# Moving a sum away from its products on VectorE, and holding back GpSimd's negations

## The chip, the cores and the metric

The kernel runs on one core of a Trainium2 chip. The metric is the device time of one execution in microseconds (us). Times are medians over several executions. A profile is one execution taken with the hardware profiler; its span is some 1.8 us shorter than the device time of the same execution.

Engines: PE is TensorE (matmuls), DVE is VectorE, ACT is ScalarE, POOL is GpSimd, SP issues DMAs.

## The reference, cut to what matters

```python
x = A_x                                              # 1 x 2048 x 576, bf16
# a 2-D Fourier filter of the normalised input, as a residual
X = rfft2(layernorm(x));  X = X * (w_r + 1j * w_i)   # 2048 x 289 complex weights
h = x + irfft2(X).astype(bf16)
# a gated feed-forward block of width 4608
h2 = h + (gelu(layernorm(h) @ w_gate) * (layernorm(h) @ w_up)) @ w_down
```

## The kernel before

The transforms are matmuls with tables. After a first stage (layer norm, table scaling, a transform along the 2048 axis) the data falls into 16 groups. In the loop over groups each group goes through five steps:

- D, on TensorE: the 576 axis, even and odd columns apart. ScalarE copies the even half out of PSUM.
- the butterfly, on VectorE: even + odd, then even - odd. Here called its sum part and its difference part.
- B, on TensorE: four-way combination of the two. ScalarE copies the result `YS` (real and imaginary plane) out of PSUM.
- the filter, on VectorE: two products of `YS` with planes of the weights `WS`, then their sum `ZS`. The first product needs a negated copy of the imaginary weights, plane 0 of `WS`. GpSimd makes these copies, one group at a time.
- V, on TensorE: the start of the inverse transform, from `ZS`. ScalarE copies the result out.

```python
def st_D(i):                      # group i: D, ScalarE's copy, then the butterfly
    ...                           # six matmuls into two banks, one ScalarE copy into ES
    P.op(DVE, ... CUS[:, s3, :, 0:HK] = e2 + o2 ...)             # L606
    P.op(DVE, ... CUS[:, s3, :, K2-1:HK-1:-1] = e2 - o2 ...)     # L607

def st_B(i):                      # group i: B, ScalarE's copy, then the filter
    ...                           # six matmuls, one ScalarE copy into YS
    for t_, w_ in enumerate((slice(1, None, -1), slice(2, 0, -1))):
        P.op(DVE, ... TP[:, sl, t_] = YS[:, sl] * WS[:, g, w_] ...)   # L629, two products
    P.op(DVE, ... ZS[:, z3] = TP[:, sl, :, 0] + TP[:, sl, :, 1] ...)  # L631, their sum

for i in range(NG):               # 16 negations on GpSimd, L665
    P.op(POOL, ... WS[:, g, 0, :] = WS[:, g, 2, :] * -1.0 ...,
         r=[imaginary weights of this half] + ["Wz"], w=[("Wn", i)])
for i in range(NG + 4):
    if i < NG:          st_D(i)
    if 2 <= i < NG + 2: st_B(i - 2)
    if i >= 4:          st_V(i - 4)
```

Each engine runs its own operations in program order. Between operations of one engine that depend on each other the program sets a semaphore wait; that holds for VectorE too. The imaginary weights arrive in two halves of eight groups, so the negations run in two blocks of eight. Right before the loop, VectorE scales the last four of sixteen table tiles (`ATS`, L472) and evicts the last results of the first stage (`U`, L505).

Of the kernel before, what the change touches and what calls it, by code (L numbers as in the profile page):

```python
# [7 lines left out]
ALU = mybir.AluOpType  # L8

S, D, K2 = 2048, 576, 289  # L10
KW = 290
# [3 lines left out]
NT = 16  # L15
NG = 16
# [279 lines left out]
def _build(nc, A_x, A_w_r, A_w_i, B_w_gate, B_w_up, B_w_down, out):  # L296
    P = Prog(nc)
    T = build_tables()
    dram = {n: nc.inline_tensor(_np_bf16(T[n]), name="c_" + n.lower()) for n in T}
    PE, DVE, ACT, SP, POOL = "pe", "dve", "act", "sp", "pool"  # L300
# [11 lines left out]
    WS = sb.alloc("WS", [128, NG, 3, KW], BF16)  # L312
# [34 lines left out]
    ATS = sb.alloc("ATS", [128, NT, 128], BF16)  # L347
# [7 lines left out]
    YS = sb.alloc("YS", [128, 2, 2, KW], BF16)  # L355
    t1_off = sb.off
    TP = sb.alloc("TP", [128, 2, 2, 2, KW], BF16)
    ZS = sb.alloc("ZS", [128, 3, 2, ZW], BF16)
# [11 lines left out]
    def bank(b, p0=0, p1=128, c0=0, c1=512):  # L370
        return PS[p0:p1, b * 512 + c0:b * 512 + c1]

    def banks(b, n, w):
        return PS[:, b * 512:(b + n) * 512].rearrange("p (a c) -> p a c", a=n)[:, :, 0:w]
# [41 lines left out]
    GORD = list(range(1, NG)) + [0]  # L416
    wkeys = [[("W", hf, pl, h) for pl in range(2) for h in range(8 + 2 * hf)] for hf in range(2)]
# [172 lines left out]
    def dbank(i):  # L590
        return 6 if i == 2 else 2 * ((i if i < 2 else i - 3) % 2)

    def st_D(i):
        g = GORD[i]
        sl, b0, s3 = i % 2, dbank(i), i % 3
        for o in range(2):
            b = b0 + o
            for dt in range(3):
                us = (2 * o + dt) if dt < 2 else 4
                P.op(PE, lambda t, b=b, o=o, dt=dt, us=us, g=g: t.matmul(bank(b, 0, 128, 0, 2 * HK), U[:, us, g, :, :], FT[:, o, dt, :],  # L600
                                                                        start=(dt == 0), stop=(dt == 2)),
                     r=uk[us] + ["FT"], w=[("PS", b)])
        P.op(ACT, lambda a, sl=sl, b0=b0: a.activation(ES[:, sl, :], bank(b0, 0, 128, 0, 2 * HK), ACTF.Copy), r=[("PS", b0)], w=[("E", sl)])
        e2 = ES[:, sl, :].rearrange("p (a b) -> p a b", a=2)
        o2 = bank(b0 + 1, 0, 128, 0, 2 * HK).rearrange("p (a b) -> p a b", a=2)
        P.op(DVE, lambda v, e2=e2, o2=o2, s3=s3: v.tensor_tensor(CUS[:, s3, :, 0:HK], e2, o2, op=ALU.add), r=[("E", sl), ("PS", b0 + 1)], w=[("CU", s3)])  # L606
        P.op(DVE, lambda v, e2=e2, o2=o2, s3=s3: v.tensor_tensor(CUS[:, s3, :, K2 - 1:HK - 1:-1], e2[:, :, 0:HK - 1], o2[:, :, 0:HK - 1], op=ALU.subtract),  # L607
             r=[("E", sl), ("PS", b0 + 1)], w=[("SU", s3)])

    LAST = NG - 1  # L610

    def st_B(i):
        g = GORD[i]
        sl = i % 2
        s3, sp_ = i % 3, 1 if g == 0 else 0
        b0 = {1: 6, LAST - 1: 2}.get(i, 4)

        for b, tabs in ((b0, (0, 1, 3)), (b0 + 1, (1, 2, 0))):
            for m, (tb, pl, q0, q1) in enumerate(((tabs[0], 0, 0, K2), (tabs[1], 1, 0, HK), (tabs[2], 1, HK, K2))):
                P.op(PE, lambda t, b=b, tb=tb, pl=pl, q0=q0, q1=q1, m=m, s3=s3, sp_=sp_: t.matmul(  # L620
                    bank(b, 0, 128, q0, q1), BT[:, sp_, tb, :], CUS[:, s3, pl, q0:q1], start=(m == 0), stop=(m == 2)),
                    r=[("CU", s3), ("SU", s3), "BT"], w=[("PS", b)])
        P.op(ACT, lambda a, sl=sl, b0=b0: a.activation(YS[:, sl, :, 0:K2], banks(b0, 2, K2), ACTF.Copy), r=[("PS", b0), ("PS", b0 + 1)], w=[("Y", sl)])  # L623
        wk = wkeys[0 if 1 <= g < 9 else 1] + [("Wn", i), "Yz", "Zz"]
        z3 = i % 3

        for q0, q1, hs in ((0, 128, (0,)), (128, KW, (1,))) if i == LAST else ((0, KW, (0, 1)),):
            for t_, w_ in enumerate((slice(1, None, -1), slice(2, 0, -1))):
                P.op(DVE, lambda v, sl=sl, g=g, q0=q0, q1=q1, t_=t_, w_=w_: v.tensor_tensor(TP[:, sl, t_, :, q0:q1], YS[:, sl, :, q0:q1], WS[:, g, w_, q0:q1], op=ALU.mult),  # L629
                     r=[("Y", sl)] + wk, w=[("T", sl, t_, h) for h in hs])  # L630
            P.op(DVE, lambda v, sl=sl, z3=z3, q0=q0, q1=q1: v.tensor_tensor(ZS[:, z3, :, q0:q1], TP[:, sl, :, 0, q0:q1], TP[:, sl, :, 1, q0:q1], op=ALU.add),  # L631
                 r=[("T", sl, t_, h) for t_ in range(2) for h in hs], w=[("Z", z3, h) for h in hs])


    VBANKS = {NG - 4: (0, 0, 1), NG - 2: (2, 2, 3), LAST: (0, 1, 4)}
# [1 line left out]
    def st_V(i):  # L637
        g = GORD[i]
        sl = i % 3
        sp_ = 1 if g == 0 else 0  # L640
        bs = VBANKS.get(i, (6, 6, 7))
        for c in range(3):
            b, o = bs[c], 256 if c == 1 and bs[0] == bs[1] else 0
            for zp in range(2):
                P.op(PE, lambda t, b=b, o=o, c=c, zp=zp, sl=sl, sp_=sp_: t.matmul(bank(b, 0, 128, o, o + 256), ZS[:, sl, zp, 128 * c:128 * c + 128],  # L645
                                                                                  VT[:, sp_, zp, :], start=(zp == 0), stop=(zp == 1)),
                     r=[("Z", sl, int(c > 0)), "Zz", "VT"], w=[("PS", b)])
            if i == LAST:
                src = bank(b, 0, 128, 0, 256).rearrange("p (k n e) -> p k n e", k=2, n=16)
                if c < 2:  # L650
                    P.op(DVE, lambda v, g=g, c=c, src=src: v.tensor_copy(V[:, 2 * c:2 * c + 2, :, g, :], src), r=[("PS", b), "Vfree"], w=[("V", g, c)])  # L651
                else:
                    P.op(ACT, lambda a, g=g, c=c, src=src: a.activation(V[:, 2 * c:2 * c + 2, :, g, :], src, ACTF.Copy), r=[("PS", b), "Vfree"], w=[("V", g, c)])
        if i < LAST:
            src = PS[:, bs[0] * 512:bs[0] * 512 + 768].rearrange("p (k n e) -> p k n e", k=6, n=16)
            P.op(ACT, lambda a, g=g, src=src: a.activation(V[:, :, :, g, :], src, ACTF.Copy), r=[("PS", bs[0]), ("PS", bs[2]), "Vfree"], w=[("V", g, c) for c in range(3)])  # L656

    def idle_ft(n, b):
        for _ in range(n):
            P.op(PE, lambda t, b=b: t.matmul(bank(b, 0, 128, 0, 2 * HK), FT[:, 0, 0, 0:128], FT[:, 0, 0, :], start=True, stop=True), r=["FT"], w=[("PS", b)])  # L660
# [2 lines left out]
    P.alias(["J0", "J1", "ZD"] + [(n_, c) for n_ in ("ATB", "ATS") for c in range(NT)], ["Vfree"])  # L663
    for i in range(NG):
        P.op(POOL, lambda v, g=GORD[i]: v.tensor_scalar(WS[:, g, 0, :], WS[:, g, 2, :], -1.0, None, op0=ALU.mult),  # L665
             r=[k for k in wkeys[0 if 1 <= GORD[i] < 9 else 1] if k[2] == 1] + ["Wz"], w=[("Wn", i)])
    for i in range(NG + 4):
        if i < NG:
            st_D(i)
        if 2 <= i < NG + 2:  # L670
            st_B(i - 2)
        if i == NG + 3:
            idle_ft(3, 5)
        if i >= 4:
            st_V(i - 4)
# [214 lines left out]
def bass_sequential_preLN__spectral_gfnet__geglu_ffn__prompt_kernel(  # L890
    nc, A_x, A_w_r, A_w_i, B_x, B_w_gate, B_w_up, B_w_down, out
):
    _build(nc, A_x, A_w_r, A_w_i, B_w_gate, B_w_up, B_w_down, out)
# [28 lines left out]
```

## Time and profile before

| | before |
|---|---|
| device time, first 3 runs | 504.44 us (504.13 to 504.98) |
| span of the profile | 502.9 us |
| first stage, ends with the first D matmul | 20.3 us |
| loop over groups | 20.3 to about 55 us |
| rest of the inverse transform | to about 77 us |
| gate, up and down matmuls | to the end |

The head of the page gives the busy time of each engine, its share of the span and its instructions; part 4 gives the chain of work that ended last, by engine.

```profile
span 502.9 us, 9972 instructions
PE 492.4 (98%) x4318; PEld 297.7 (59%) x4319; DVE 183.9 (37%) x391; ACT 158.7 (32%) x296; POOL 39.1 (8%) x49
...
PE 91%; DVE 6%; issue 1%; DMA 1%; ACT 1%; DVEq 0%
```

TensorE is busy nearly all the time, and the reader may stop there. But 6% of the chain, some 30 us, belongs to VectorE. Some 13 us of it lie in the first stage and some 17 us in the loop over groups. The next lines are VectorE's timeline of the kernel before, one group of the loop. The columns are start in us, length in us, engine, line, operation, output and inputs, shapes, count, and in brackets the idle time before it where there is any.

```profile
27.59 0.45 DVE L606 TENSOR_TENSOR CUS<-ES,PS 128x290 bf16<-128x290 f32 x1
27.96 0.45 DVE L607 TENSOR_TENSOR CUS<-ES,PS 128x288 bf16<-128x288 f32 x1
28.32 0.83 DVE L629 TENSOR_TENSOR TP<-YS,WS 128x580 bf16<-128x580 bf16 x2
29.18 0.47 DVE L631 TENSOR_TENSOR ZS<-TP 128x580 bf16<-128x580 bf16 x1
29.56 0.45 DVE L606 TENSOR_TENSOR CUS<-ES,PS 128x290 bf16<-128x290 f32 x1
```

Look at starts, not lengths. The butterfly's two parts start 0.37 us apart (27.59, 27.96), though each lasts 0.45 us: neighbours overlap. The two products end at 28.32 + 0.83 = 29.15 us, and the sum that reads them starts only then, at 29.18. A sum that could overlap would have started about 0.11 us earlier. This lost overlap, where an operation reads what the one right in front of it wrote, is called the drain below. One group takes 29.56 - 27.59 = 1.97 us, without a pause. This time from group to group is called the pitch.

TensorE needs 0.75 + 0.51 + 0.65 = 1.91 us for D, B and V of a group, read from starts where nothing holds it up. So in the middle of the loop VectorE is the tighter of the two by only 0.06 us. At the end of the loop, TensorE stands and waits for the sums (TensorE's timeline of the kernel before):

```profile
50.00 1.03 PE L645 MATMUL PS<-VT,ZS 128*128 128x256 bf16 x6 [0.64 <-DVE ZS L631]
50.87 0.67 PE L620 MATMUL PS<-CUS,BT 128*128 128x289 bf16 x6
51.97 0.82 PE L645 MATMUL PS<-VT,ZS 128*128 128x256 bf16 x6 [0.43 <-DVE ZS L631]
53.12 0.83 PE L645 MATMUL PS<-VT,ZS 128*128 128x256 bf16 x6 [0.33 <-DVE ZS L631]
```

The other place is the last table scaling before the loop. These lines are from VectorE's and GpSimd's timelines of the kernel before:

```profile
17.14 0.26 DVE L472 TENSOR_SCALAR ATS<-ATB,RS 128x128 bf16<-128x128 bf16 x1
17.60 0.79 DVE L472 TENSOR_SCALAR ATS<-ATB,RS 128x128 bf16<-128x128 bf16 x3 [0.21 <-issue]
17.75 0.97 POOL L665 TENSOR_SCALAR WS<-WS 128x290 bf16<-128x290 bf16 x1 [2.05 <-DMA WS<-in_A_w_i_dram]
```

The last three scalings take 0.79 us together, and there is a hole of 0.21 us before them. A negation on GpSimd starts at 17.75 us, when its weights land.

### The profile page before, as it was taken

What the parts mean: (1) busy time and instruction counts of PE and PEld (TensorE: products, weight loads), DVE (VectorE), ACT (ScalarE), POOL (GpSimd) and SP (SyncE); (2) the same over time, 40 slices, a digit from 0 to 9 for tenths busy, and PEclk for the clock granted to TensorE, in tenths of its full rate; (3) what the DMA queues carried; (4) which work ended last, traced back from release to release, by engine and by line L of the source; (5) the groups of instructions that cost most, each with busy time, mean ns of one, the idle gap of its engine ahead of it and who ended that gap; (6) DMA issues with size and microseconds to landing.
All of it is one profiled execution on the core that took longest, in us unless ns stands there. A gap on an engine that the chain in (4) does not pass through costs nothing.

```text
span 502.9 us, 9972 instructions
## 1 busy us (share of the span) xinstructions
PE 492.4 (98%) x4318; PEld 297.7 (59%) x4319; DVE 183.9 (37%) x391; ACT 158.7 (32%) x296; POOL 39.1 (8%) x49
## 2 busy tenths in 40 slices
PE   6899999999999999999999999999999999999998
PEld 2687674444458764444477744444577644444775
DVE  5899673344431114343310134333201233333111
ACT  7888776653220003333200023323100133323000
POOL 3644281000000000000000000000000000000000
PEclk9999999999999999999999999999999999999999
DMA  8779789001100000100000001100000000000000
GB/s 284 165 224 334 235 292 353 6 4 25 25 5 13 18 19 17 22 17 1 2 7 18 19 15 23 22 4 1 1 18 19 13 1 1 1 2 2 12 19 19
DMA packets 25948, 28.64 MB, mean 57 GB/s; under 512 B 11568, under 2 KB 19888, under 8 KB 25776
## 3 DMA queue, kind: packets, MB, share of 16 engines
q1 hardware_dynamic: 23328, 17.39, 12.1%
q0 software_dynamic: 2576, 10.62, 6.3%
q8 instruction: 34, 0.56, 0.5%
q14 instruction: 10, 0.08, 0.1%
HBM read 23.66 MB, written 2.36 MB: 52 GB/s over the span
## 4 chain that ended last, share of the span: by engine, by line
PE 91%; DVE 6%; issue 1%; DMA 1%; ACT 1%; DVEq 0%
PE PS L838 56%; PE PS L861 28%; PE PS L700 3%; DVE TP L629 2%; PE PS L739 2%; PE PS L600 1%; DVE ST L440 1%; DVE CUS L606 1%; PE PS L645 1%; DVE CUS L607 1%; DMA XO<-in_A_x_dram 1%; PE PS L620 1%; DVE U L505 0%; DVE ATS L472 0%; ACT JNK L431 0%
## 5 line engine op out<-in xcount | busy, mean ns | idle before, releaser
L838 PE MATMUL PS<-HT,WGU 64*128 64x512 bf16 x2592 | 281.9, 376 | 0.0
L838 PEld LDWEIGHTS PS<-HT,WGU 64*128 64x128 bf16 x2592 | 137.3, 94 | 143.4 <-issue 1.2
L850 ACT ACTIVATE GL<-PS 128x512 bf16<-128x512 f32 x144 | 85.9, 597 | 289.3 <-PE PS L838 289.3
L851 DVE TENSOR_TENSOR AT<-GL,PS 128x512 bf16<-128x512 bf16 x144 | 99.0, 688 | 174.1 <-PE PS L838 172.5
L861 PE MATMUL PS<-WD,AT 128*128 128x288 bf16 (+2 forms) x1152 | 141.8, 286 | 0.0
L861 PEld LDWEIGHTS PS<-WD,AT 128*128 128x128 bf16 x1152 | 111.0, 98 | 31.5 <-issue 1.7
L864 DVE TENSOR_TENSOR OS<-PS,XO 128x288 bf16<-128x288 f32 (+2 forms) x32 | 14.7, 458 | 125.8 <-PE PS L861 125.8
L665 POOL TENSOR_SCALAR WS<-WS 128x290 bf16<-128x290 bf16 x16 | 15.2, 949 | 9.3 <-DMA WS<-in_A_w_i_dram 8.2
L742 DVE SCALAR_TENSOR_TENSOR XO<-PS,XO 128x576 bf16<-128x576 f32 x16 | 12.1, 756 | 8.4 <-PE PS L739 8.4
L645 PE MATMUL PS<-VT,ZS 128*128 128x256 bf16 x96 | 13.4, 272 | 1.7 <-DVE ZS L631 1.4
L600 PE MATMUL PS<-FT,U 128*128 128x290 bf16 x96 | 14.4, 287 | 0.5 <-DVE U L505 0.5
L700 PE MATMUL PS<-DT,V 128*128 128x289 bf16 x96 | 14.6, 287 | 0.2 <-DVE V L651 0.2
L629 DVE TENSOR_TENSOR TP<-YS,WS 128x580 bf16<-128x580 bf16 (+2 forms) x34 | 13.5, 438 | 0.3 <-issue 0.3
L656 ACT ACTIVATE V<-PS 128x768 bf16<-128x768 f32 x15 | 12.2, 811 | 2.1 <-PE PS L645 1.8
L623 ACT ACTIVATE YS<-PS 128x578 bf16<-128x578 f32 x16 | 10.5, 655 | 3.3 <-PE PS L620 3.3
L494 PE MATMUL PS<-ATS,XO 128*128 128x128 bf16 (+1 forms) x80 | 7.1, 223 | 4.4 <-POOL ATS L467 2.7
L709 ACT ACTIVATE GS<-PS 128x578 bf16<-128x578 f32 x15 | 9.8, 655 | 4.2 <-PE PS L700 4.1
L645 PEld LDWEIGHTS PS<-VT,ZS 128*128 128x128 bf16 x96 | 8.1, 97 | 4.8 <-DVE ZS L631 1.0
L600 PEld LDWEIGHTS PS<-FT,U 128*128 128x128 bf16 x96 | 9.2, 98 | 3.0 <-issue 0.7
L700 PEld LDWEIGHTS PS<-DT,V 128*128 128x128 bf16 x96 | 8.9, 97 | 3.4 <-DVE V L651 0.4
L730 ACT ACTIVATE OS<-XO 128x576 bf16<-128x576 bf16 x16 | 10.8, 675 | 0.0
L620 PE MATMUL PS<-CUS,BT 128*128 128x289 bf16 (+2 forms) x96 | 10.7, 247 | 0.0
(58 smaller groups left out, 158.6 us busy)
## 6 DMA issues: line engine op xcount, KB each, us to landing
WD<-in_B_w_down_dram POOLq DMA_DIRECT2D x9, 576.0 KB, 8.3
WGU<-in_B_w_up_dram SPq DMA_DIRECT2D x4, 1152.0 KB, 9.6
WGU<-in_B_w_gate_dram POOLq DMA_DIRECT2D x4, 1152.0 KB, 10.4
out_dram<-OS SPq DMA_DIRECT2D x30, 72.0 KB, 1.6
XO<-in_A_x_dram SPq DMA_DIRECT2D x3, 576.0 KB, 6.9
IT<-c_itab SPq DMA_DIRECT2D x1, 1024.0 KB, 7.0
HT<-HN SPq DMA_TRANSPOSE x60, 2.4
XO<-in_A_x_dram SPq DMA_DIRECT2D x2, 288.0 KB, 3.2
```

The lines of the kernel that those rows point to most:

```text
L600: P.op(PE, lambda t, b=b, o=o, dt=dt, us=us, g=g: t.matmul(bank(b, 0, 128, 0, 2 * HK), U[:, us, g, :, :], FT[:, o, dt, :], start=(dt == 0) ...
L620: P.op(PE, lambda t, b=b, tb=tb, pl=pl, q0=q0, q1=q1, m=m, s3=s3, sp_=sp_: t.matmul(bank(b, 0, 128, q0, q1), BT[:, sp_, tb, :], CUS[:, s3, ...
L629: P.op(DVE, lambda v, sl=sl, g=g, q0=q0, q1=q1, t_=t_, w_=w_: v.tensor_tensor(TP[:, sl, t_, :, q0:q1], YS[:, sl, :, q0:q1], WS[:, g, w_, q ...
L645: P.op(PE, lambda t, b=b, o=o, c=c, zp=zp, sl=sl, sp_=sp_: t.matmul(bank(b, 0, 128, o, o + 256), ZS[:, sl, zp, 128 * c:128 * c + 128], VT[ ...
L656: P.op(ACT, lambda a, g=g, src=src: a.activation(V[:, :, :, g, :], src, ACTF.Copy), r=[("PS", bs[0]), ("PS", bs[2]), "Vfree"], w=[("V", g, ...
L665: P.op(POOL, lambda v, g=GORD[i]: v.tensor_scalar(WS[:, g, 0, :], WS[:, g, 2, :], -1.0, None, op0=ALU.mult), r=[k for k in wkeys[0 if 1 <= ...
L700: P.op(PE, lambda t, b=b, h=h, i=i, kt=kt, c=c: t.matmul(bank(b, 0, 128, 0, K2), V[:, kt, c, :, :], DT[:, 3 * h + i, 0:K2], start=(i == 0) ...
L838: op = P.op(PE, lambda t, h0=h0, kt=kt, wt=wt, f=f, b=b, HT=HT, s=(half == 0 and j in (0, 5)), e=(half == 1 and j in (3, 8)): t.matmul(ban ...
L850: P.op(ACT, lambda a, s2=s2, b0=b0: a.activation(GL[:, s2, :], bank(b0), ACTF.Gelu_apprx_tanh), r=[("PS", b0)], w=[("GL", s2)])
L851: P.op(DVE, lambda v, s2=s2, b0=b0, f=f: v.tensor_tensor(AT[:, f, :], GL[:, s2, :], bank(b0 + 1), op=ALU.mult), r=[("GL", s2), ("PS", b0 + ...
L861: P.op(PE, lambda t, b=b, d0=d0, d1=d1, f=f, p=p: t.matmul(bank(b, 0, 128, 0, d1 - d0), AT[:, f, 128 * p:128 * p + 128], WD[:, f, d0:d1], ...
L864: P.op(DVE, lambda v, b=b, d0=d0, d1=d1, p=p, c=c: v.tensor_tensor(OS[:, p % 2, d0:d1], bank(b, 0, 128, 0, d1 - d0), XO[:, c, d0:d1], op=A ...
```

## The change

It has two parts. First, the sum of group i-3 goes between the butterfly's two parts of group i, so that it no longer follows the product it reads. The end of the loop is reordered in the same spirit. Second, GpSimd's negations must wait until the last table tile is scaled.

```diff
-        (butterfly at the end of st_D)
+    def st_U(i):
         P.op(DVE, ... CUS[:, s3, :, 0:HK] = e2 + o2 ...)
+        if i >= 3:
+            st_Z(i - 3)
         P.op(DVE, ... CUS[:, s3, :, K2-1:HK-1:-1] = e2 - o2 ...)
-        (products and sum at the end of st_B)
+    def st_T(i, t_, ...):   # one product
+    def st_Z(i, ...):       # the sum
...
     for i in range(NG):
         P.op(POOL, ... WS[:, g, 0, :] = -WS[:, g, 2, :] ...,
-             r=[...] + ["Wz"], w=[("Wn", i)])
+             r=[...] + ["Wz", ("ATS", NT - 1)], w=[("Wn", i)])
     for i in range(NG + 4):
         if i < NG:
             st_D(i)
+            st_U(i)
+        if i == NG:
+            st_Z(NG - 3)
         if 2 <= i < NG + 2:
             st_B(i - 2)
+        if 2 <= i <= NG:
+            st_T(i - 2, 0)
+            st_T(i - 2, 1)
+        if i == NG + 1:
+            (products of the last group by halves, between them the last two groups' sums)
         ...
```

No operation is added or removed.

More of the change, by code (lines that the diff above doesn't have):

```diff
@@ L603, in st_D @@
         P.op(ACT, lambda a, sl=sl, b0=b0: a.activation(ES[:, sl, :], bank(b0, 0, 128, 0, 2 * HK), ACTF.Copy), r=[("PS", b0)], w=[("E", sl)])
+    def st_U(i):
+        sl, b0, s3 = i % 2, dbank(i), i % 3
         e2 = ES[:, sl, :].rearrange("p (a b) -> p a b", a=2)
@@ L623, in st_B, with st_T, st_Z @@
         P.op(ACT, lambda a, sl=sl, b0=b0: a.activation(YS[:, sl, :, 0:K2], banks(b0, 2, K2), ACTF.Copy), r=[("PS", b0), ("PS", b0 + 1)], w=[("Y", sl)])
-        wk = wkeys[0 if 1 <= g < 9 else 1] + [("Wn", i), "Yz", "Zz"]
-        z3 = i % 3
-        for q0, q1, hs in ((0, 128, (0,)), (128, KW, (1,))) if i == LAST else ((0, KW, (0, 1)),):
-            for t_, w_ in enumerate((slice(1, None, -1), slice(2, 0, -1))):
-                P.op(DVE, lambda v, sl=sl, g=g, q0=q0, q1=q1, t_=t_, w_=w_: v.tensor_tensor(TP[:, sl, t_, :, q0:q1], YS[:, sl, :, q0:q1], WS[:, g, w_, q0:q1], op=ALU.mult),
-                     r=[("Y", sl)] + wk, w=[("T", sl, t_, h) for h in hs])
-            P.op(DVE, lambda v, sl=sl, z3=z3, q0=q0, q1=q1: v.tensor_tensor(ZS[:, z3, :, q0:q1], TP[:, sl, :, 0, q0:q1], TP[:, sl, :, 1, q0:q1], op=ALU.add),
-                 r=[("T", sl, t_, h) for t_ in range(2) for h in hs], w=[("Z", z3, h) for h in hs])
+    def st_T(i, t_, q0=0, q1=KW, hs=(0, 1)):
+        g, sl = GORD[i], i % 2
+        w_ = (slice(1, None, -1), slice(2, 0, -1))[t_]
+        P.op(DVE, lambda v: v.tensor_tensor(TP[:, sl, t_, :, q0:q1], YS[:, sl, :, q0:q1], WS[:, g, w_, q0:q1], op=ALU.mult),
+             r=[("Y", sl), ("Wn", i), "Yz", "Zz"] + wkeys[0 if 1 <= g < 9 else 1], w=[("T", sl, t_, h) for h in hs])
+    def st_Z(i, q0=0, q1=KW, hs=(0, 1)):
+        sl, z3 = i % 2, i % 3
+        P.op(DVE, lambda v: v.tensor_tensor(ZS[:, z3, :, q0:q1], TP[:, sl, :, 0, q0:q1], TP[:, sl, :, 1, q0:q1], op=ALU.add),
+             r=[("T", sl, t_, h) for t_ in range(2) for h in hs], w=[("Z", z3, h) for h in hs])
     VBANKS = {NG - 4: (0, 0, 1), NG - 2: (2, 2, 3), LAST: (0, 1, 4)}
@@ L665, in _build @@
         P.op(POOL, lambda v, g=GORD[i]: v.tensor_scalar(WS[:, g, 0, :], WS[:, g, 2, :], -1.0, None, op0=ALU.mult),
-             r=[k for k in wkeys[0 if 1 <= GORD[i] < 9 else 1] if k[2] == 1] + ["Wz"], w=[("Wn", i)])
+             r=[k for k in wkeys[0 if 1 <= GORD[i] < 9 else 1] if k[2] == 1] + ["Wz", ("ATS", NT - 1)], w=[("Wn", i)])
     for i in range(NG + 4):
@@ L669, in _build @@
             st_D(i)
+            st_U(i)
+        if i == NG:
+            st_Z(NG - 3)
         if 2 <= i < NG + 2:
             st_B(i - 2)
+        if 2 <= i <= NG:
+            st_T(i - 2, 0)
+            st_T(i - 2, 1)
+        if i == NG + 1:
+            st_T(LAST, 0, 0, 128, (0,))
+            st_Z(LAST - 1)
+            st_T(LAST, 1, 0, 128, (0,))
+            st_T(LAST, 0, 128, KW, (1,))
+            st_Z(LAST, 0, 128, (0,))
+            st_T(LAST, 1, 128, KW, (1,))
+            st_Z(LAST, 128, KW, (1,))
         if i == NG + 3:
```

## The prediction

> **What bounds the kernel now.** The page gives TensorE 98% of a 502.9 us span; its chain is 91% TensorE, 56% and 28% of it the gate/up and down matmuls, which the change does not touch. Only the spectral filter, about 20.3 to 55.6 us, can gain. There the chain of waits runs on VectorE from 33.7 to 54.6 us. In the timeline one group takes VectorE five operations: butterfly sum, butterfly difference, two filter products, their sum. Independent neighbours start 0.37 us apart though each lasts 0.45 us: they overlap by 0.08 us. The sum, which waits for the second product, starts only 0.03 us after that one's end. So a group takes 1.97 us (27.59, 29.56, 31.53 us) and VectorE has no idle time. TensorE needs, undisturbed, 0.75 + 0.51 + 0.65 = 1.91 us per group, ScalarE less.
>
> The Trainium skill, "VectorE: DVE Perf Modes", section "The DRAIN you can't avoid", says that the next operation waits for the pipe to empty and that a semaphore costs nothing. This trace differs: 0.37 us between independent starts, 0.48 us where the next reads the result.
>
> **What the change does.** It removes no work. It puts the sum of group i-3 between two operations that do not depend on it, so the drain of about 0.11 us goes, once per group: VectorE 1.97 -> 1.86 us. Then TensorE is the limit, 1.91 us, so in the steady state 0.06 us per group is won on TensorE's side, while VectorE catches up. The second inverse-stage operand comes one group later, about 0.15 us once at the start; later there is slack. In the tail (48.7 to 55.2 us), where TensorE waits 0.64 + 0.43 + 0.33 us for the sums, VectorE's lead counts in full: 16 drains x 0.11 = 1.8 us. Sum for the loop: about 1.8 us.
>
> Second part: GpSimd's negations start at 17.75 us, beside the last four table scalings on VectorE. These take 17.14 to 18.39 us with a hole of 0.21 us, one of them 0.456 us; the first ones took 0.25 us at a pitch of 0.17. Undisturbed: 0.76 instead of 1.25 us. The chain runs through them (scalings, evictions, first filter matmul at 20.33 us), so about 0.4 us. The negations then start near 18 us; their first user is at 24 us, so they are not late. The Trainium skill, "SBUF — State Buffer", section "SBUF: two separate sides", describes an exclusive lock between GpSimd and VectorE operations with two SBUF inputs or in a two-port mode. The trace agrees in direction, not in a full block: the sum takes 0.56 to 0.62 us beside the second block of negations (32.0 to 40.2 us), 0.46 us without, and groups take 2.07 us there. That block waits for a DMA, so it stays; I expect still some 2.0 us per group there.
>
> **On the critical path:** both parts, fully; from 55 us on the matmul stages are bound by TensorE and should only shift. 1.8 + 0.4 = 2.2 us, less a little for new hitches: 2.1 us, 504.44 -> 502.3 us. Range 501.5 to 503.7. Faster by over 2% would need 10 us: chance 0.005; within 2%: 0.99; slower: 0.005.
>
> **What would show it.** Sums no longer 0.48 us after the second product; groups at 1.91 us on TensorE from 26 to 32 and 41 to 47 us, VectorE with small gaps; first filter matmul near 19.9 us; last sum ends near 52.2 instead of 54.6 us; first gate/up matmul near 74.6 instead of 76.8 us; everything after unchanged in length.
>
> **What would make it wrong.** Negations blocking the sums or products longer at their new place; the scaling's hole having another cause; TensorE now waiting for the later sum in every group; ScalarE's queue delaying the tail; weight loads arriving too late for the earlier start.

## More of the kernel before

One run of the kernel before, of 574.59 us, was slow and is left out everywhere.

## The result, and the profile after

| | before | after |
|---|---|---|
| device time, 4 runs each | 504.71 us (504.13 to 505.09) | 502.91 us (502.74 to 503.11) |
| first D matmul | 20.33 us | 20.17 us |
| first V matmul | 25.85 us | 25.73 us |
| V of the twelfth group | 48.04 us | 47.11 us |
| last filter sum ends | 54.63 us | 52.82 us |
| first gate/up matmul | 76.72 us | 75.03 us |
| span of the profile | 502.9 us | 501.2 us |

The ratio is 0.9965, with a 95% interval of 0.9948 to 0.9983. A ratio here is the mean time of one kernel's runs over that of the other's runs of the same rounds, so it is not quite the ratio of the medians quoted. Executions over 1.5% slower than the fastest of the same kernel are left out of the means. The interval excludes 1: 1.8 us are gained.

The table shows where, for these two profiles. 0.16 us come before the loop, of which 0.04 are lost again up to the first V. These 0.16 us need not be the change's: in the profile of order_only below, which has no new wait, the first D began at 20.11 us, and in that of wait_only at 19.98 us. Between the first V and the twelfth 0.81 us are gained, from there to the last sum another 0.88 us. After the loop everything moves along: the first gate/up matmul is 1.69 us earlier and the span 1.7 us shorter.

The page's head after:

```profile
span 501.2 us, 9972 instructions
PE 492.9 (98%) x4319; PEld 299.5 (60%) x4319; DVE 182.5 (36%) x391; ACT 158.4 (32%) x296; POOL 39.8 (8%) x49
...
PE 90%; DVE 7%; issue 1%; DMA 1%; SPq 0%; ACT 0%; DVEq 0%
```

It tells next to nothing: a gain of 0.35% does not show in shares. VectorE's timeline of the kernel after, one group, does:

```profile
28.60 0.44 DVE L610 TENSOR_TENSOR CUS<-ES,PS 128x290 bf16<-128x290 f32 x1
28.97 0.45 DVE L640 TENSOR_TENSOR ZS<-TP 128x580 bf16<-128x580 bf16 x1
29.34 0.44 DVE L613 TENSOR_TENSOR CUS<-ES,PS 128x288 bf16<-128x288 f32 x1
29.71 0.81 DVE L635 TENSOR_TENSOR TP<-YS,WS 128x580 bf16<-128x580 bf16 x2
30.45 0.44 DVE L610 TENSOR_TENSOR CUS<-ES,PS 128x290 bf16<-128x290 f32 x1
```

All five operations now start 0.37 us after the one before. A group takes 30.45 - 28.60 = 1.85 us, 0.12 us less. TensorE waits less at the end of the loop, 0.22 + 0.35 + 0.47 us where it waited 0.64 + 0.43 + 0.33 us:

```profile
48.66 0.83 PE L654 MATMUL PS<-VT,ZS 128*128 128x256 bf16 x6 [0.22 <-DVE ZS L640]
49.32 0.67 PE L626 MATMUL PS<-CUS,BT 128*128 128x289 bf16 x6
50.35 0.82 PE L654 MATMUL PS<-VT,ZS 128*128 128x256 bf16 x6 [0.35 <-DVE ZS L640]
51.63 0.83 PE L654 MATMUL PS<-VT,ZS 128*128 128x256 bf16 x6 [0.47 <-DVE ZS L640]
```

Before the loop, the three scalings are back at 0.58 us and the negation starts after them. The hole of 0.2 us is still there, with nothing running on GpSimd:

```profile
17.20 0.25 DVE L472 TENSOR_SCALAR ATS<-ATB,RS 128x128 bf16<-128x128 bf16 x1
17.65 0.58 DVE L472 TENSOR_SCALAR ATS<-ATB,RS 128x128 bf16<-128x128 bf16 x3 [0.19 <-issue]
...
18.39 0.97 POOL L674 TENSOR_SCALAR WS<-WS 128x290 bf16<-128x290 bf16 x1 [2.63 <-DVE ATS L472]
```

### The profile page after: what moved, and what is told of

Same layout as the page of the kernel before. It is cut to its first block, busy times and chain, and to the rows that moved or that the text cites. A ratio compares the mean times of both kernels' runs of the same rounds, so it can differ in the third digit from the quotient of the medians.

```text
span 501.2 us, 9972 instructions
## 1 busy us (share of the span) xinstructions
PE 492.9 (98%) x4319; PEld 299.5 (60%) x4319; DVE 182.5 (36%) x391; ACT 158.4 (32%) x296; POOL 39.8 (8%) x49
## 4 chain that ended last, share of the span: by engine, by line
PE 90%; DVE 7%; issue 1%; DMA 1%; SPq 0%; ACT 0%; DVEq 0%
PE PS L861 56%; PE PS L884 28%; PE PS L723 3%; DVE TP L635 2%; PE PS L762 2%; DVE ST L440 1%; DMA XO<-in_A_x_dram 1%; DVE ZS L640 1%; DVE CUS L613 1%; PE PS L600 1%; DVE U L505 0%; SPq L206 0%; PE PS L807 0%; PE PS L654 0%; DVE CUS L610 0%
## 5 line engine op out<-in xcount | busy, mean ns | idle before, releaser
L762 PE MATMUL PS<-GS,IT 128*128 128x288 bf16 x64 | 10.5, 285 | 0.0
L483 PE MATMUL PS<-ZD 128*128 128x512 bf16 x24 | 9.1, 537 | 1.3 <-POOL ZD L377 1.3
```

Of the source, the lines that this page charges most:

```text
L762: P.op(PE, lambda t, b=b, h=h, i=i, c=c, rhs=rhs: t.matmul(bank(b, 0, 128, 0, 288), IT[:, h * i, c, :], rhs, start=(i == 0), stop=(i == 1) ...
```

## The experiments

Twelve kernels ran, in three sets; each set shares its runs of the kernel before (medians of the fast ones 504.60, 504.57 and 504.81 us). All gave the right result but one.

| kernel | device time, median | ratio to before, 95% interval |
|---|---|---|
| order_only | 502.95 us | 0.9967 (0.9955 to 0.998) |
| wait_only | 504.62 us | 0.9997 (0.9984 to 1.001) |
| drain_back | 504.15 us | 0.999 (0.9978 to 1.0003) |
| sum_after_difference | 502.99 us | 0.9968 (0.9954 to 0.9981) |
| no_negation (wrong result) | 502.19 us | 0.9953 (0.994 to 0.9965) |
| batched_negation | 507.16 us | 1.0051 (1.0037 to 1.0065) |
| vector_negation | 502.85 us | 0.9967 (0.9954 to 0.9979) |
| four_extra_ops | 502.93 us | 0.9968 (0.9954 to 0.9981) |
| late_sum_from_8 | 503.29 us | 0.9966 (0.9953 to 0.9979) |
| late_sum_and_half_on_vector | 502.39 us | 0.9956 (0.9942 to 0.997) |
| vector_negation_fewer | 502.79 us | 0.9963 (0.995 to 0.9976) |
| early_plane (one run) | 503.18 us | not timed |

### Each part alone: order_only and wait_only

order_only is the kernel after without the new wait:

```diff
-             r=[...] + ["Wz", ("ATS", NT - 1)], w=[("Wn", i)])
+             r=[...] + ["Wz"], w=[("Wn", i)])
```

> The new order of VectorE's operations alone, the negations free to start as before. Theory D (the sum no longer waits for the drain of the product right before it): nearly all of the gain is here, about 1.5 of 1.8 us, so about 503.1 us against 504.7; the group's pitch on VectorE where GpSimd is idle is 1.84 us instead of 1.97. Rival P (the gain comes from GpSimd's negations starting later, so that they no longer disturb VectorE): no more than 0.3 us here, about 504.4 us.

wait_only is the kernel before with that wait:

```diff
-             r=[...] + ["Wz"], w=[("Wn", i)])
+             r=[...] + ["Wz", ("ATS", NT - 1)], w=[("Wn", i)])
```

> The old order with the negations made to wait for the last table scaling. Theory D: about 0.2 us, as the chain from the first scaling of the last group (17.20 us) to the first filter matmul (20.17 us) took 2.97 us after the change and 3.19 before; total about 504.5 us, pitch of a group 1.97 us where GpSimd is idle. Rival P: most of the 1.8 us, about 503.1 us. The forecast of 0.4 us for this part fails if the hole of 0.2 us between the first two of these scalings is still there.

The order alone gives 502.95 us, the whole gain as far as these runs can tell. The wait alone gives 504.62 us, nothing that these runs can see; the interval would hide some 0.2 us. Rival P falls. In the profile of order_only the weights landed a little later than in that of before, at 18.14 us, as the last scaling ended (18.17 us). So there was nothing for the wait to prevent. The pitch of a group where GpSimd is idle was 1.84 us in order_only and 1.97 us in wait_only, as expected. In wait_only the hole was there too, and its first negation started later, at 18.21 us. VectorE's and GpSimd's timelines of order_only:

```profile
17.59 0.58 DVE L472 TENSOR_SCALAR ATS<-ATB,RS 128x128 bf16<-128x128 bf16 x3 [0.21 <-issue]
18.14 8.47 POOL L674 TENSOR_SCALAR WS<-WS 128x290 bf16<-128x290 bf16 x8 [2.45 <-DMA WS<-in_A_w_i_dram]
```

VectorE's timeline of wait_only:

```profile
17.46 0.58 DVE L472 TENSOR_SCALAR ATS<-ATB,RS 128x128 bf16<-128x128 bf16 x3 [0.19 <-issue]
```

### The drain put back: drain_back

The second product of group i-3 is moved right in front of its sum. The sum keeps its new place in the loop.

```diff
         if i >= 3:
+            st_T(i - 3, 1)
             st_Z(i - 3)
...
         if i == NG:
+            st_T(NG - 3, 1)
             st_Z(NG - 3)
...
             st_T(i - 2, 0)
-            st_T(i - 2, 1)
+            if i == NG:
+                st_T(i - 2, 1)
```

> The kernel after the change, with the second product of group i-3 moved to stand right in front of its sum, between the butterfly's two parts. The sum keeps its new place and its lateness, but again reads what the operation right before it wrote. Theory D: the drain is back, the pitch is 1.95 to 1.97 us where GpSimd is idle, and the time about 504.4 us, like wait_only. Rival O (the place of the sum matters: later for TensorE, between two operations that read PSUM): the pitch stays 1.84 us and the time 502.9 us.

VectorE's timeline of drain_back, one group (L636 is a product, L641 the sum, L610 and L614 the butterfly):

```profile
28.23 0.46 DVE L610 TENSOR_TENSOR CUS<-ES,PS 128x290 bf16<-128x290 f32 x1
28.60 0.46 DVE L636 TENSOR_TENSOR TP<-YS,WS 128x580 bf16<-128x580 bf16 x1
29.09 0.46 DVE L641 TENSOR_TENSOR ZS<-TP 128x580 bf16<-128x580 bf16 x1
29.47 0.45 DVE L614 TENSOR_TENSOR CUS<-ES,PS 128x288 bf16<-128x288 f32 x1
29.83 0.46 DVE L636 TENSOR_TENSOR TP<-YS,WS 128x580 bf16<-128x580 bf16 x1
30.20 0.45 DVE L610 TENSOR_TENSOR CUS<-ES,PS 128x290 bf16<-128x290 f32 x1
```

Here product and sum stand apart and can be read singly. Every start is 0.36 to 0.38 us after the one before, but the sum starts 29.09 - 28.60 = 0.49 us after its product, at the product's end. The group is back at 1.97 us and the time at 504.15 us. From the first D to the last sum the loop took 53.95 - 19.95 = 34.00 us, as in wait_only (34.07 us), against 32.46 us in order_only. Rival O, that the place of the sum matters, falls. The 0.45 us by which the time is under before lie within the interval of the timing, so nothing is read from them.

The semaphore wait as such is not what costs. In the trace of the kernel after, the sum still carries a wait for VectorE's own semaphore, but for a product that ended earlier, and it starts 0.37 us after its neighbour. What costs 0.11 us is to wait for the operation right in front.

### Another independent neighbour: sum_after_difference

```diff
         P.op(DVE, ... even + odd ...)
-        if i >= 3:
-            st_Z(i - 3)
         P.op(DVE, ... even - odd ...)
+        if i >= 3:
+            st_Z(i - 3)
```

> The kernel after the change, with the sum of group i-3 behind the butterfly's difference instead of in front of it. It depends on neither. Theory D: any independent neighbour will do, the pitch stays 1.84 us and the time is within 0.3 us of 502.9. Rival O: the place between the two parts matters, so the gain shrinks by half or more, 503.8 us or over. Beside the negations the three operations with two SBUF inputs now stand in a row; if the lost time is per first one of such a row, the group beside the second block of negations gets no slower than 1.98 us.

502.99 us: another independent neighbour does as well. The pitch is 1.84 us. The profile showed something else, though. While the second block of negations ran, VectorE kept this pitch from 32.1 to 39.5 us, as if GpSimd were not there, and the eight negations took 11.36 us where they take 8.81 us in the kernel after. Here the time was lost on GpSimd's side. That led to the third set. What was won there was lost elsewhere in the same profile: the first V started at 25.84 us, 5.93 us after the first D; in the kernel after it was 25.73 - 20.17 = 5.56 us.

### What the negations still cost: no_negation

The negations are left out, and the first product reads a plane of right shape and wrong sign. The relative error was 0.042.

```diff
-    for i in range(NG):
-        P.op(POOL, ... negation ...)
...
-        w_ = (slice(1, None, -1), slice(2, 0, -1))[t_]
+        w_ = (slice(1, 3), slice(2, 0, -1))[t_]
...   (GpSimd's weight loads: r=list(wkeys[1]) added)
```

> Wrong result on purpose: the kernel after the change with GpSimd's 16 negations left out (the first product reads a plane of right shape and wrong sign; GpSimd's weight loads are tied to the second half of the filter's imaginary plane, so that they start near 32 us). It sizes what the negations still cost after the change. Theory C (they still hold up VectorE, 0.88 us in all beside five groups in the profile after, 0.73 of it in the second block): the pitch is 1.84 us until TensorE bounds it at 1.91, and the time falls by 0.5 to 0.8 us to about 502.2. Rival T (TensorE at 1.91 us per group bounds the stage already, so VectorE's lost time is slack): within 0.2 us of 502.9.

502.19 us, and all five runs lie within 0.06 us. So the negations cost the changed kernel 502.91 - 502.19, about 0.7 us (medians of two sets). In the profiles 0.61 us of it lie in the loop: from the first D to the last sum it took 32.04 us, against 32.65 us. Theory C holds. In this profile TensorE runs at 1.91 us per group through the whole loop, and after the first groups VectorE waits for ScalarE's copy only once, near 50 us.

### One long negation: batched_negation

```diff
-    for i in range(NG):
-        P.op(POOL, ... one group ...)
+    for g0, g1 in ((1, 9), (9, 16), (0, 1)):
+        P.op(POOL, ... groups g0 to g1 ...)
```

> The kernel after the change with three negations (8, 7 and 1 groups) in place of 16, the same elements. Theory L (GpSimd holds the shared port for its whole instruction and VectorE's two-input operations block): the 7-group negation of some 2 to 4 us stalls a product for over 1 us at one go near 32 to 36 us, and the time is no better than 502.9. Rival S (a negation holds VectorE up only for a short part of itself, 0.1 to 0.24 us per meeting as in the profile after): fewer instructions mean fewer meetings, no stall over 0.3 us, time 502.3 to 502.7.

507.16 us in the median, worse than before. From the timeline of batched_negation, both engines:

```profile
32.41 5.33 POOL L674 TENSOR_SCALAR WS<-WS 128x2030 bf16<-128x2030 bf16 x1 [8.21 <-DMA WS<-in_A_w_i_dram]
32.45 0.46 DVE L610 TENSOR_TENSOR CUS<-ES,PS 128x290 bf16<-128x290 f32 x1
...
32.82 3.53 DVE L640 TENSOR_TENSOR ZS<-TP 128x580 bf16<-128x580 bf16 x1
```

The sum, which reads two tiles in SBUF, takes 3.53 us instead of 0.46 us. The butterfly part in front of it has one input in PSUM and is not touched. Theory L holds and rival S falls: GpSimd keeps VectorE's two-input operation out for most of a long instruction. The short negations of the kernel after take 0.94 us each, and VectorE pays 0.1 to 0.25 us a time beside them. That this is the same exclusion, only shorter, fits but is not shown. The first product also had to wait longer for the first negation (start 24.33 us, 24.01 us after the change). The profiled run was the quickest of its five, 505.50 us; the others took 506.94 to 507.27 us. Why these are slower by another 1.5 us was not looked into.

### The negations on VectorE: vector_negation and vector_negation_fewer

Groups 1 to 8 are negated in one operation while VectorE waits for the first D matmuls, the others between later groups, in three operations and in two.

```diff
-    (16 negations on POOL)
+    neg(1, 9)                                         # DVE, ahead of the loop
...
+        (vector_negation)       at i = 8, 10, 12: neg(9, 13), neg(13, 16), neg(0, 1)
+        (vector_negation_fewer) at i = 9, 13:     neg(9, 16), neg(0, 1)
...   (GpSimd's weight loads: r=list(wkeys[1]) added, as in no_negation)
```

> The kernel after the change with the negations moved to VectorE: 8 groups in one operation in the 0.7 us in which it waits for the first filter matmuls (20.6 to 21.3 us), the rest in three operations between the products of later groups. GpSimd does nothing beside the filter stage. [...]the other three cost about 0.75 us, about what the second block of negations costs after the change (0.73 us), so 502.6 to 503.0 us.[...]

> vector_negation with the second half in two operations in place of three (7 groups and 1). The three cost 0.37 + 0.37 + 0.15 = 0.89 us of VectorE; two should cost about 0.75 if the 7-group one runs in the fast mode like the 8-group one: 502.7 us against vector_negation's 502.85. If it falls to half speed for its odd number of rows: about 1.3 us and 503.2 us.

502.85 and 502.79 us, both about as good as the kernel after. The first operation took 0.76 us and delayed nothing: the butterfly of the first group started 1.16 us after the first D, as it did after the change. The others cost VectorE about what GpSimd's interference had cost. The longer operation of the second variant took 0.75 us for seven rows of 290, as much as the 0.76 us for eight. So it ran at the pace of the 8-row operation, which is what the expectation calls the fast mode, but the missing row saved nothing. The two medians are too close together to tell the variants apart.

### The hole before the scalings: four_extra_ops

```diff
+    for _ in range(4):
+        P.op(DVE, lambda v: v.memset(OS[:, 0, 0:4], 0.0), ...)   # first on VectorE
```

> The kernel after the change with four tiny memsets at the very start of VectorE's program, where it waits for the first DMA anyway. The hole of 0.19 to 0.21 us between the first and second scaling of the last group stands in every run so far, with and without negations beside it. Theory F (it belongs to a position in VectorE's instruction stream): the hole moves four instructions earlier, ahead of the scalings, and the time stays 502.9 us. Rival W (it belongs to these scalings, what they read or wait for): it stays between the first and second scaling.

VectorE's timeline of four_extra_ops:

```profile
15.95 0.15 DVE L452 SCALAR_TENSOR_TENSOR MV<-SA,TM 128x1 f32<-128x1 f32 x1
16.38 0.69 DVE L505 CAST U<-PS 128x512 bf16<-128x512 f32 x1 [0.28 <-PE PS L494]
...
17.26 0.74 DVE L472 TENSOR_SCALAR ATS<-ATB,RS 128x128 bf16<-128x128 bf16 x4
```

The four scalings now run without a hole, in 0.74 us. A hole of 0.28 us stands in front of the eviction, which is four instructions earlier in the program; the profile puts it down to TensorE, for which the eviction waits. It was not TensorE: this eviction is of the third group of table tiles, whose matmuls ran from 12.75 to 14.27 us in the same profile. So the hole moved with the position in VectorE's instruction stream. Theory F holds, and neither the time (502.93 us) nor the start of the loop changes. In all fourteen traces the hole comes after the 63rd instruction that is recorded for VectorE, counting waits and the two records before its first operation. What the machine does there is not shown.

### Does order decide which engine waits: late_sum_from_8 and late_sum_and_half_on_vector

In both, the sum stands behind the difference part from group 8 on. In the second, the first eight negations are one VectorE operation ahead of the loop; GpSimd makes the other eight.

```diff
-        if i >= 3:
+        if 3 <= i < 8:
             st_Z(i - 3)
         P.op(DVE, ... even - odd ...)
+        if i >= 8:
+            st_Z(i - 3)
```

> The kernel after the change, with the sum behind the butterfly's difference from group 8 on only, that is beside the second block of negations. In sum_after_difference the pitch stayed 1.84 us there up to 39.5 us while the negations themselves were stretched (11.36 us for eight, 8.81 after the change), and two products were held up, not four. If the order of VectorE's operations decides which engine waits, the same happens here without that kernel's later start of the inverse stage: 502.4 to 502.7 us. If that was chance: 502.9 us.

> The same, with the first eight negations as one VectorE operation in the time in which it waits for the first filter matmuls (0.76 us in vector_negation, with no later start of the group behind it). It takes away the one meeting of the first block, 0.15 us on VectorE: 0.1 to 0.2 us under late_sum_from_8, about 502.4 us. A candidate to beat both kernels; no_negation puts the floor of it at 502.2 us.

late_sum_from_8 took 502.40 and 502.55 us in two runs and 503.29 to 503.46 us in three. The profile is of a slow one of these (503.46 us). late_sum_and_half_on_vector took 502.17 to 502.43 us in four runs and 503.25 us in one; its profile is of a quick one. The pair of products of one group beside the second block of negations, first in late_sum_from_8:

```profile
35.31 1.05 DVE L637 TENSOR_TENSOR TP<-YS,WS 128x580 bf16<-128x580 bf16 x2
```

and in late_sum_and_half_on_vector:

```profile
34.98 0.82 DVE L637 TENSOR_TENSOR TP<-YS,WS 128x580 bf16<-128x580 bf16 x2
```

The groups of negations on GpSimd in the same two profiles, in the same order:

```profile
32.21 8.49 POOL L676 TENSOR_SCALAR WS<-WS 128x290 bf16<-128x290 bf16 x8 [5.81 <-DMA WS<-in_A_w_i_dram]
```

```profile
32.56 13.26 POOL L678 TENSOR_SCALAR WS<-WS 128x290 bf16<-128x290 bf16 x8 [16.93 <-DMA WS<-in_A_w_i_dram]
```

Eight negations in 8.49 us cost VectorE 0.23 us in each of four groups (pitch 2.07 us). Eight in 13.26 us, which is 1.66 us each, cost it nothing: every pair of products takes 0.82 us and the pitch stays 1.84 us. So there are two rhythms: either VectorE waits for GpSimd or GpSimd for VectorE. That one and the same code has both is inferred: the times of each of these kernels fall into two groups some 0.8 us apart, but each kernel was profiled in one of them alone. My expectation named the order as what decides, and that fell for late_sum_from_8: the same kernel shows both times. What tips it is open. It may be the moment at which the weights land, which lay 0.35 us apart in the two profiles, but nothing here shows it.

late_sum_and_half_on_vector has the lowest median of the correct kernels. Its median is 502.39 us, against 502.91 us for the kernel after, and 502.19 us with no negations at all. One run in five was in the worse rhythm, and the kernel after was timed in another set, so the 0.5 us are a difference of medians across sets; the intervals of the two ratios to before overlap.

### What the wait guards against: early_plane

order_only, with the first half of the imaginary weights loaded ahead of the tables `FT`, `BT`, `VT`:

```diff
+    for f in w_loads(1, 0, SP):
+        f()
     P.dma(SP, FT ...); P.dma(SP, BT ...); P.dma(SP, VT ...)
-    for f in w_loads(1, 0, SP) + w_loads(0, 0, SP) + ...:
+    for f in w_loads(0, 0, SP) + ...:
```

> order_only with the first half of the filter's imaginary plane loaded ahead of the three tables, so that the negations, which do not wait for the scaling here, start before it, near 16 us. Theory: negations beside the last four scalings lengthen them, the last three from 0.58 us to 0.79 us (as in the profile of before, where a negation started at 17.75 us) or more, which is what the wait of the change guards against. Rival: the 0.79 us there had another cause, and they take 0.58 us here too. The total time is not of interest, as the tables come later.

VectorE's and GpSimd's timelines of early_plane:

```profile
17.27 0.25 DVE L474 TENSOR_SCALAR ATS<-ATB,RS 128x128 bf16<-128x128 bf16 x1
17.73 0.79 DVE L474 TENSOR_SCALAR ATS<-ATB,RS 128x128 bf16<-128x128 bf16 x3 [0.20 <-issue]
...
15.76 8.20 POOL L676 TENSOR_SCALAR WS<-WS 128x290 bf16<-128x290 bf16 x8 [0.17 <-POOL ATS L469]
```

With negations running from 15.76 us on, the three scalings take 0.79 us again, as in the profile of before, and 0.58 us in all profiles where no negation runs beside them. So the guard has something to prevent: 0.2 us on VectorE in an execution in which the weights land early enough. It was one run; only the lengths are read from it.

## Why the prediction was right or wrong

The forecast was 502.3 us in a range of 501.5 to 503.7; measured were 502.91 us. The step was forecast as 2.1 us and came out as 1.8 us.

**Right: the drain is the mechanism of the order's gain.** "The sum, which waits for the second product, starts only 0.03 us after that one's end": the pitch fell from 1.97 to 1.85 us (forecast 1.86), drain_back brought it back to 1.97 us and the time with it, and sum_after_difference kept it with another neighbour.

**Right: TensorE at 1.91 us per group, and the rest of the gain in the tail.** D starts at 28.37, 30.29 and 32.20 us after the change, 1.91 us apart. Of the loop's gain about half was made before the twelfth V and half after it.

**Right, roughly: the groups beside the second block.** Forecast "some 2.0 us per group". From 32.29 to 40.41 us four groups took 8.12 us, 2.03 us each.

**Slightly too large, and right by some luck: "16 drains x 0.11 = 1.8 us" for the loop.** From the first D to the end of the last sum, the loop took 54.63 - 20.33 = 34.30 us before and 52.82 - 20.17 = 32.65 us after, 1.65 us less. There were 17 sums, the last group's in two halves. In the new tail two of them still directly follow their own product (group 13, and the second half of the last group), so 15 drains went. That 15 x 0.11 is 1.65 as well is partly luck. The pitch fell by 0.12 to 0.13 us, so 15 of them are worth some 1.8 us: the count was one too high, the size a little too low. What took the sum down to 1.65 us is a greater loss beside the negations, by some 0.2 us: from the first to the 14th group's products VectorE took 26.33 us before and 24.88 us after. That is 0.72 us more than 13 undisturbed pitches of 1.97 us before, and 0.90 us more than 13 of 1.845 us after. All of these are estimates from the two profiles.

**Mis-sized: "Undisturbed: 0.76 instead of 1.25 us. ... so about 0.4 us" for the scalings.** This is the term that failed. The hole of 0.21 us was put down to the negations and is not theirs: it stands in wait_only and after the change with GpSimd idle, and four_extra_ops moved it with the instruction stream. The other half, 0.79 instead of 0.58 us, is theirs (early_plane), but only in executions in which the weights land before the scalings end. In the timed runs the wait alone gave 504.62 against 504.60 us; their interval alone would not rule 0.4 us out, the place of the hole does. The milestones came 0.27 to 0.62 us later than forecast: the first D at 20.17 us (forecast 19.9), the last sum's end at 52.82 (52.2), the first gate/up matmul at 75.03 (74.6).

**Wrong in a detail: "VectorE with small gaps".** VectorE was busy for 6.00 of 6.00 us between 26 and 32 us. It starts the loop behind TensorE, its pitch is only 0.06 us shorter than TensorE's, and the second block of negations pushed it back by some 0.7 us. So it never caught up. Without negations it did, near 50 us.

**Foreseen only as a risk: the interference moved.** Before, it was the sum that took 0.56 to 0.62 us beside the negations. After, it is mostly the pair of products, 0.97 to 1.05 us instead of 0.82. The loss did not vanish; no_negation sizes it at 0.7 us.

## What to carry to other kernels

On an engine that never idles, compare the start of an operation with the end of the one before: where a result is read by the very next operation, the overlap is lost, here 0.11 us each time, and an independent operation put between them won it back at no cost in both places tried. Before giving a hole to a suspected neighbour, look for the hole in a run without that neighbour. Work that one engine did here in the background for another did least harm in short instructions (0.1 to 0.25 us a meeting, against 3.07 us for a long one) or where VectorE did it itself in its idle time (no delay seen); where the two met periodically, the times of the same code fell into two groups, so look at single times and not only at the median.

## What the Trainium skill lacked or had wrong

- "VectorE: DVE Perf Modes", section "The DRAIN you can't avoid", says that the next operation does not start until the pipe is empty, but also that one that is not held starts earlier. Here the second holds: independent operations of 0.45 us started 0.37 us apart. The section found that a semaphore costs nothing extra, and the rules for kernel authors say to keep the number of operations small and not to mind semaphores. What is lacking is that it matters which operation is waited for: 0.48 to 0.49 us from start to start where it is the one right in front, 0.37 us where it ended earlier, with a wait in both cases. The count of operations stayed, and the loop became 1.65 us shorter.
- "SBUF — State Buffer", section "SBUF: two separate sides", has the exclusive lock between GpSimd and VectorE operations with two SBUF inputs. batched_negation agrees in kind: a sum of 3.53 us instead of 0.46 us. It was let in before the negation's recorded end, though (36.35 us against 37.74 us; spans on GpSimd are rough). That the loss can fall on either side follows from the section, which gives the lock to whichever starts first. What it lacks is that with short instructions the loss can stay on one side for a whole block: eight negations took 8.49 us and cost VectorE 0.23 us per group, or took 13.26 us and cost it nothing.
- The same section counts a VectorE operation in a two-port mode among those that lock. The table scalings, with one tile in SBUF as input, were held up too: 0.79 us for three beside a negation, 0.58 us without. That agrees if they ran in such a mode, which no run shows.
- "VectorE: DVE Perf Modes", in its section on the TRN2 errata, finds a fixed term of about 150 cycles. It agrees: an estimate from that page, 2320 elements at 4 per cycle and 0.96 GHz plus 150 cycles, is 0.76 us, and vector_negation's operation of eight rows took 0.76 us. Seven rows took 0.75 us and three rows 0.48 us, as long as eight (0.76 us) and four (0.47 us).
- No page that was consulted has the hole of about 0.2 us in VectorE's instruction stream, after its 63rd recorded instruction, in all fourteen profiles.
